# A gated S4D layer on one core: kernel tables finished in place in a wider tile, wider VectorE operations, tokens put in order on GpSimd

## The chip, the core and the metric

The kernel runs on one core of one Trainium2 chip. The metric is device microseconds for one execution; the time before is the median of three runs. TensorE (PE) does the matmuls, VectorE (DVE), ScalarE (ACT) and GpSimd (POOL) the elementwise work, and SyncE (SP), ACT and POOL issue the DMAs. All arithmetic is fp32; matmuls written on `F32R` tiles take one pass over the columns, and the others are plain fp32. To keep accuracy with `F32R`, an operand is split into a rounded part ("high") and the rest ("low"), and a product is made of high×high, high×low and low×high.

## What is computed

`x` is 2048 tokens of 576 channels. After a LayerNorm two branches run on the same `xn`, and their product is added to `x`:

```python
xn = layernorm(x)
s  = S4D(xn)                       # long convolution per channel
g  = silu(MLP(xn))                 # 576 -> 4608 -> 576, per token, with its own layernorm
return x + s * g

# S4D: the convolution kernel K[d, l], l = 0..2047, from 128 complex states per channel
A = -exp(log_A_real) + 1j * A_imag;  C = (C_real + 1j * C_imag) * dt
K = 2 * real(einsum("dn,dnl->dl", C, exp(A * dt * l)))
y = irfft(rfft(xn, 4096) * rfft(K, 4096))[:2048] + xn * D_skip

# MLP
h = gelu(layernorm(xn) @ w1 + b1);   out = h @ w2 + b2
```

## The kernel before

**The MLP is the frame.** The hidden width 4608 goes in 12 groups of 384, and the tokens in 4 blocks of 512; a *slot* is one block with one group, and there are 48 slots. A slot has 3 positions of layer 1 (`layer1`, L599, 13 or 14 matmuls of 512 columns each) and 8 of layer 2 (`layer2`, L662, 72 matmuls of 288 columns). Between the two, ACT takes the GELU (L635) and the high part (L638) and DVE the low part (L641, tile `hl`); after layer 2 DVE adds the block to `acc` (L672). The weights of the next group are split by ACT and DVE (L552, L549).

**The S4D branch is put between these matmuls.** The 576 channels go in 36 batches of 16 for the convolution kernel and in 6 chunks of 96 for the transform:

- `tables(b)`, one batch of 16 channels: tile `w` (2 x 16 x 65 columns, two buffers) takes a phase for 65 time steps per channel (DVE L897, L900, L906; ACT L903, L909), then its cosine and sine (ACT L914, L916). `mags` (L922) makes magnitudes in `mg`. `weigh` multiplies them: six operations of 512 columns write the single-buffered tiles `U` (2 x 16 x 32) and `v` (2 x 16 x 64) (L933, L935, L937, L939). The phase of batch b waits until the `weigh` of batch b-2 is done, and the first `weigh` of batch b until the outer product of batch b-1 is done.
- `kgen(b)`, the **outer product** (L978): 32 fp32 matmuls of 64 columns on 128x32 tiles of TensorE, weights from `U`, columns from `v`. It gives K at 2048 places for 16 channels, which ACT copies to `kt` (L983).
- `chunk(c)`, the transform in steps: `x1` (L1082, from the tokens), `k1` (L1113, from `kt`), four times `s2` (L1143, both at once), the pointwise complex product, two inverse steps (L1185), the last inverse step `i1` (L1211). Between them DVE transposes (L1090, L1121, L1196).
- `in_parts` splits the input of `x1` and `k1`: ACT high (L1058), DVE low (L1062). For `x1` both read the tile `xc` (32 tokens x 24 channels a partition) with tokens and channels exchanged, so that neighbours lie 96 bytes apart; for `k1` they read `kt` as it lies.
- The pointwise product in `s2`: `copy` (ACT L1152) takes the kernel's half of PSUM to `kk`; `prod` (DVE L1158) makes two products of 384 columns, and `sums` (L1164, L1165) a difference and a sum of 192 columns.

**Order.** `Order` is a planner that runs while the program is recorded. It has a time for each engine, a price for each step (`dve(n)`, `act(n)`, written-out numbers) and steps in lines, and it records steps in the order of its own times; the order on each engine is then fixed. Work that layer 2 waits for has a due time (`hidden_by`, `look_ahead`), and other work goes ahead of it only if it ends before that. `pe_turns` decides which S4D step goes to TensorE at a position of a slot. A step of a chunk is taken when its inputs have been ready for 0.4 us by the plan and, for `x1`, `k1` and `s2`, when some share of the mean distance between steps has passed.

**Company.** `ride` lets an outer product that is ready go right ahead of a step `x1`, `k1`, `s2` or `i1` (its *host*), in columns 384 to 511 of the host's PSUM tile (`lead`). An outer product that found no host goes alone once it has been ready for `ALONE` = 12 us, or 3 us when the next batch's sines are made and its due time (from 160 to 950 us, spread over the batches) has passed; in `pe_turns`:

```python
wait = ("sin", b + 1, 1) not in od.marks or od.t["PE"] < DUE[0] + b * (DUE[1] - DUE[0]) / NB
if b < NB - 1 and od.t["PE"] < h[1] + (ALONE if wait else 3.0):
    break
```

**A pair.** The last 64 rows of layer 1's input can be worked for two positions at once on two 64-row halves of TensorE (`pair`, L582). It is used at the end of a slot if an S4D step follows there and its operands are in time; it saves the two matmuls on `w1s` that the next slot would have.

Of the kernel before, what the change touches and what calls it, by code (L numbers as in the profile page):

```python
# [210 lines left out]
def mixer_kernel(ctx, tc, u, log_a_real, a_imag, c_real, c_imag, log_dt, d_skip, w1, b1, w2, b2,  # L211
# [38 lines left out]
    idp = sb.tile([P, P], F32, name="idp")  # L250
# [112 lines left out]

    def table_memory():

        t = [sb.tile([P, 2, SB, NV], F32, name="w", bufs=2) for _ in range(2)]
        t = [x.rearrange("p k c t -> p (k c t)") for x in t + [sb.tile([P, 2, SB, 64], F32, name="v")]]
        return [t[k // 3][:, k % 3 * D:(k % 3 + 1) * D] for k in range(8)]
# [401 lines left out]
    def params():  # L770
# [8 lines left out]
        dt = sb.tile([P, 2, SB, 32], F32, name="U").rearrange("p a b c -> p (a b c)")[:, :D]  # L779
# [108 lines left out]
    def tables(b):  # L888
# [5 lines left out]
        def phase(k):  # L894
            if k == 0:
                T["w"] = sb.tile([P, 2, SB, NV], F32, name="w", bufs=2)
                nc.vector.tensor_mul(T["w"][:, 1], bc(PAR[b][:, :, 0], 2, NV), bc(tv, 1, SB))  # L897
            else:
                u = T["w"][:, 1, :, 33:]
                nc.vector.tensor_add(u, u, bc(PAR[b][:, :, 1], 2, 32))  # L900
# [24 lines left out]
        def weigh(k, part):  # L925

            if k == 0 and part == 0:
                T["v"] = sb.tile([P, 2, SB, 64], F32, name="v")
                T["U"] = sb.tile([P, 2, SB, 32], F32, name="U")
                TAB[b] = (T["U"], T["v"])  # L930
            w, v, m = T["w"], T["v"], T["m"]
            if part == 0:
                nc.vector.tensor_mul(T["U"][:, k], w[:, k, :, 33:], m[:, :, 64:])  # L933
            elif part == 1:
                nc.vector.tensor_mul(v[:, k, :, :32], w[:, k, :, 32:0:-1], m[:, :, :32])  # L935
            elif k == 0:
                nc.vector.tensor_mul(v[:, k, :, 32:], w[:, k, :, :32], m[:, :, 32:64])  # L937
            else:
                nc.vector.scalar_tensor_tensor(v[:, k, :, 32:], w[:, k, :, :32], -1.0, m[:, :, 32:64],  # L939
# [6 lines left out]
                 step("DVE", dve(SB * NV), f(phase, 0), need=[("wu", b - 2, 1)] if b > 1 else []),  # L946
# [6 lines left out]
                + [step("DVE", dve(n), f(weigh, k, part), need=[("sin", b, k)] + ([("kg", b - 1)] if b else []),  # L953
                        mark=("wu", b, k) if part == 2 else None) for k in range(2) for part in range(3)])
# [10 lines left out]
    def kgen(b):  # L965
# [20 lines left out]
        return [step("PE", KG + 0.2, mm, need=need + [("wu", b, 1)], cv=1, mark=("kg", b)),  # L986
# [23 lines left out]
    def chunk(c):  # L1010
# [41 lines left out]
        def in_parts(which, i, get, m, need):  # L1052

            def high():
                a = sb.tile([P, 2, 4 * CH], F32R, name="pr").rearrange("p t c -> p (t c)")
                b = sb.tile([P, 2, 4 * CH], F32R, name="ys", bufs=2).rearrange("p t c -> p (t c)")
                PARTS2[which, i] = [t.rearrange("p (c b) -> p c b", b=m) for t in (a, b)]
                nc.scalar.activation(PARTS2[which, i][0], get(), AF.Copy)  # L1058

            def low():  # L1060
                a, b = PARTS2[which, i]
                nc.vector.tensor_sub(b, get(), a.bitcast(F32))  # L1062

            n = 768 if which == "k" else 2000
            four.append(step("ACT", act(n), high, need=need))
            four.append(step("DVE", dve(n), low, mark=(which + "p", c, i)))

        def x1(i):
# [641 lines left out]
```

## Time and profile before

| | |
|---|---|
| median of three runs | 1099.98 us (1099.77 to 1100.17) |
| span of the profiled execution | 1099.5 us |
| TensorE busy | 1090.1 us (99%) |
| VectorE busy | 920.5 us (84%) |
| ScalarE busy | 696.6 us (63%) |
| GpSimd busy | 184.6 us (17%) |
| DMA, mean over the span | 126 GB/s |

The times of runs are those of executions without the profiler; the trace is one profiled execution, and all places ("at 621 us") are in its own time. A row of a view names the source line, the engine, the operation, what it writes and reads, and the shape; in the views by groups there follow the count, busy time in us, mean ns of one, and the idle time of that engine just before with what ended it. In the timeline a row starts with the start time and the duration in us; equal neighbours are merged with their count. Matmuls overlap each other in their records, so the rate of TensorE is read from the starts of successive rows.

### The profile page before, as it was taken

To read this page: it belongs to the slowest core of one execution; us is meant where nothing else is said; L and a number is where in the kernel's file an instruction comes from. 1 tells how busy PE (TensorE), PEld (TensorE's weight loads), DVE (VectorE), ACT (ScalarE), POOL (GpSimd) and SP (SyncE) were. 2 spreads that over 40 slices of the span, in tenths; PEclk is the share of its full clock that TensorE was granted. 3 is DMA by queue.
4 is the path that set the end of the run, shared out by engine and by line. 5 is a ranking of instruction groups with operands and counts; after the bars stand their busy time and mean duration, and the time that the engine had idled before them with its cause. 6 is when DMAs were issued, how large, how long until landed. Compare 5 with 4: busy or idle time off the path is not lost.

```text
span 1099.5 us, 27206 instructions
## 1 busy us (share of the span) xinstructions
PE 1090.1 (99%) x11447; PEld 953.9 (87%) x11447; DVE 920.5 (84%) x1514; ACT 696.6 (63%) x1040; POOL 184.6 (17%) x254
## 2 busy tenths in 40 slices
PE   9999999999999999999999999999999999999997
PEld 7989899889888888888998888888888888888896
DVE  7798678979998899999999998898998986765356
ACT  6585699866666675676865857566675754325233
POOL 5566211170110100001100000000100012110220
PEclk9999999999999999999999999999999999999999
DMA  8746655734444152455623314242333426453453
GB/s 230 235 144 156 232 162 196 215 75 126 154 124 145 48 112 57 116 121 143 150 57 94 91 56 126 39 147 60 90 92 77 143 65 180 117 177 108 126 149 94
DMA packets 139683, 138.23 MB, mean 126 GB/s; under 512 B 88952, under 2 KB 105016, under 8 KB 138984
## 3 DMA queue, kind: packets, MB, share of 16 engines
q1 hardware_dynamic: 124664, 85.49, 29.5%
q0 software_dynamic: 14336, 50.12, 14.8%
q8 instruction: 89, 1.46, 0.6%
q10 hardware_dynamic: 560, 0.89, 0.3%
q14 instruction: 34, 0.28, 0.1%
HBM read 102.17 MB, written 36.63 MB: 126 GB/s over the span
## 4 chain that ended last, share of the span: by engine, by line
PE 96%; SPq 1%; DMA 1%; DVE 1%; issue 0%; ACT 0%; ACTq 0%; DVEq 0%
PE mxb L662 21%; PE mxa L662 21%; PE mxa L599 20%; PE mxb L599 20%; PE cv L1143 3%; PE cv L978 3%; PE cv L1185 2%; PE cv L1211 2%; PE cv L1113 1%; PE cv L1082 1%; DMA w<-in_A_u_dram 1%; SPq L791 1%; PE mxa L614 0%; SPq L383 0%; DMA acc<-in_A_u_dram 0%
## 5 line engine op out<-in xcount | busy, mean ns | idle before, releaser
L641 DVE TENSOR_TENSOR hl<-h,hh 128x512 fp32r<-128x512 f32 x144 | 99.1, 691 | 88.3 <-ACT hh L638 87.6
L662 PE MATMUL mxb<-w2h,hh 128*128 128x288 f32 x576 | 171.6, 298 | 0.0
L662 PE MATMUL mxa<-w2h,hh 128*128 128x288 f32 x573 | 170.8, 298 | 0.0
L662 PE MATMUL mxb<-w2h,hl 128*128 128x288 f32 x576 | 170.1, 295 | 0.3 <-DVE hl L641 0.3
L662 PE MATMUL mxb<-w2l,hh 128*128 128x288 f32 x576 | 169.5, 294 | 0.0
L662 PE MATMUL mxa<-w2h,hl 128*128 128x288 f32 x573 | 169.1, 295 | 0.0
L662 PE MATMUL mxa<-w2l,hh 128*128 128x288 f32 x573 | 168.6, 294 | 0.0
L635 ACT ACTIVATE h<-mxa,b1t 128x512 f32<-128x512 f32 x73 | 50.2, 688 | 111.8 <-PE mxa L599 110.1
L662 PEld LDWEIGHTS mxa<-w2h,hh 128*128 128x128 f32 x573 | 107.6, 188 | 6.6 <-issue 3.5
L662 PEld LDWEIGHTS mxb<-w2h,hh 128*128 128x128 f32 x576 | 108.1, 188 | 5.7 <-issue 1.5
L662 PEld LDWEIGHTS mxb<-w2l,hh 128*128 128x128 f32 x576 | 108.1, 188 | 0.6
L662 PEld LDWEIGHTS mxb<-w2h,hl 128*128 128x128 f32 x576 | 108.1, 188 | 0.5 <-DVE hl L641 0.5
L662 PEld LDWEIGHTS mxa<-w2l,hh 128*128 128x128 f32 x573 | 107.6, 188 | 0.6
L662 PEld LDWEIGHTS mxa<-w2h,hl 128*128 128x128 f32 x573 | 107.5, 188 | 0.0
L879 POOL DMA_DIRECT2D par<-par_s x36 | 27.8, 773 | 464.2 <-DVE mg L922 459.5
L638 ACT ACTIVATE hh<-h 128x512 fp32r<-128x512 f32 x144 | 90.6, 630 | 3.6
L635 ACT ACTIVATE h<-mxb,b1t 128x512 f32<-128x512 f32 x71 | 48.9, 689 | 68.9 <-PE mxb L599 66.5
L672 DVE TENSOR_TENSOR acc<-mxa,acc 128x576 f32<-128x576 f32 x87 | 65.5, 752 | 31.4 <-PE mxa L662 31.0
L672 DVE TENSOR_TENSOR acc<-mxb,acc 128x576 f32<-128x576 f32 x88 | 66.1, 752 | 16.0 <-PE mxb L662 15.5
L599 PE MATMUL mxa<-XH,w1h 128*128 128x512 f32 x284 | 79.1, 400 | 0.0
L599 PE MATMUL mxb<-XH,w1h 128*128 128x512 f32 x280 | 77.8, 399 | 0.0
L599 PE MATMUL mxa<-XL,w1h 128*128 128x512 f32 x284 | 76.1, 390 | 0.0
(261 smaller groups left out, 2485.9 us busy)
## 6 DMA issues: line engine op xcount, KB each, us to landing
raw<-in_B_w_dram SPq DMA_DIRECT2D x72, 288.0 KB, 3.5
raw<-in_B_w_dram SPq DMA_DIRECT2D x96, 192.0 KB, 3.8
par_s<-A POOLq DMA_DIRECT2D x4, 2160.0 KB, 8.2
par<-par_s POOLq DMA_DIRECT2D x36, 240.0 KB, 3.6
f2t<-f2q SPq DMA_DIRECT2D x24, 256.0 KB, 3.3
g2t<-g2p SPq DMA_DIRECT2D x24, 256.0 KB, 4.0
bias<-XR SPq DMA_DIRECT2D x42, 128.0 KB, 3.8
raw<-in_B_w_dram SPq DMA_DIRECT2D x48, 96.0 KB, 4.0
```

Of the source, the lines that this page charges most:

```text
L599: nc.tensor.matmul(q, a, b, start=j == 0 and i not in BEGUN, stop=j == len(ops) - 1, skip_group_check=True)
L635: nc.scalar.activation(t, q, AF.Gelu_apprx_tanh, bias=b1t[:, k:k + 1], scale=1.0)
L638: LAST[0] = nc.scalar.activation(hh[:, i], t, AF.Copy)
L641: nc.vector.tensor_sub(hl[:, i], t, hh[:, i].bitcast(F32))
L662: nc.tensor.matmul(q[:, dh, :288], a[:, i, c], b[:, i, d], start=i == 0 and k == 0 and not alone, stop=i == G - 1 and k == 2)
L672: nc.vector.tensor_add(o, q[:, dh:dh + n, :288], b)
L791: nc.sync.dma_start(r[32 * g:32 * g + 32].rearrange("c (b n) -> c b n", n=32), dram(src[k], 32 * g, [[N, 32], [32 * N, D // 32], [1, 32]]))
L879: nc.gpsimd.dma_start(PAR[b].rearrange("p (g i) k -> p g (i k)", g=4), dram(par_s, (b // 3 * 48 + b % 3 * 4) * NPAR, [[D * NPAR, P], [12 * ...
L978: nc.tensor.matmul(q[32 * g:32 * g + 32, i // 2, i % 2 * 64:i % 2 * 64 + 64], U[:, ri, 4 * g + i, :], v[:, ri, 4 * g + i, :], start=ri == ...
L1143: nc.tensor.matmul(Q[i][32 * q:32 * q + 32, f, 2 * ri:2 * ri + 2], m[r, 4 * i + q, 32 * ri:32 * ri + 32], A2[r, 4 * p + 2 * i + q // 2, :, ...
L1185: nc.tensor.matmul(QI[q // 2][64 * f:64 * f + 64, q % 2, i], MAT["g2t", p + i // 2][r, i % 2, f, ri], YS[p + i // 2][0][r, i % 2, ri, f], ...
L1211: nc.tensor.matmul(Q[h][64 * y:64 * y + 64, t], g1t.rearrange("p a e -> p (a e)"), A2[:, k:k + 2, 1].rearrange("p i d r -> p i r d"), star ...
```

## The change

- **One tile for the tables.** `w` becomes 2 x 16 x 97 columns with two buffers (`table_tile`); the phases and their cosines and sines stand in its last 65 columns, `weigh` writes its results into the same tile, and `U` and `v` are gone. The phase of batch b now waits for the outer product of batch b-2, and `weigh` no longer waits for one. The six operations of `weigh` become four: two of 1024 columns and two of 512.
- **Outer products** without a host wait 20 us by the plan (`ALONE`).
- **Wider operations.** The transposes after `x1` and `k1` take 24 channels at once (48 of 768 columns for 96 of 384). In `s2` the results of matmuls go to PSUM in another order (`ri::2`: two runs of 96 columns with 96 columns between them), `kk` gets a third, negated copy by one more ACT operation, and `prod` and `sums` become one operation each of 768 and 384 columns.
- **GpSimd orders tokens.** For `x1` a `tensor_copy` on POOL writes the exchanged tokens to a new tile `xt`; ACT high and DVE low read that as it lies.
- `idp` and the parameter tile `dt` take the memory of other tiles.

```diff
-    idp = sb.tile([P, P], F32, name="idp")
+    idp = sb.tile([P, 4, P], F32, name="f2t")[:, 0]
...
+    def table_tile():
+        return sb.tile([P, 2, SB, 32 + NV], F32, name="w", bufs=2)
...
             if k == 0:
-                T["w"] = sb.tile([P, 2, SB, NV], F32, name="w", bufs=2)
+                T["v"] = table_tile()
+                T["w"] = T["v"][:, :, :, 32:]
...
-        def weigh(k, part):
+        def weigh(part):
...
             if part == 0:
-                nc.vector.tensor_mul(T["U"][:, k], w[:, k, :, 33:], m[:, :, 64:])
+                nc.vector.tensor_mul(v[:, :, :, :32], w[:, :, :, 32:0:-1], bc(m[:, :, :32], 1, 2))
             elif part == 1:
-                nc.vector.tensor_mul(v[:, k, :, :32], w[:, k, :, 32:0:-1], m[:, :, :32])
-            elif k == 0:
-                nc.vector.tensor_mul(v[:, k, :, 32:], w[:, k, :, :32], m[:, :, 32:64])
+                nc.vector.tensor_mul(w[:, :, :, 33:], w[:, :, :, 33:], bc(m[:, :, 64:], 1, 2))
+            elif part == 2:
+                nc.vector.tensor_mul(w[:, 0, :, :32], w[:, 0, :, :32], m[:, :, 32:64])
...
-                 step("DVE", dve(SB * NV), f(phase, 0), need=[("wu", b - 2, 1)] if b > 1 else []),
+                 step("DVE", dve(SB * NV), f(phase, 0), need=[("kg", b - 2)] if b > 1 else []),
...
-                + [step("DVE", dve(n), f(weigh, k, part), need=[("sin", b, k)] + ([("kg", b - 1)] if b else []),
-                        mark=("wu", b, k) if part == 2 else None) for k in range(2) for part in range(3)])
+                + [step("DVE", dve((2, 2, 1, 1)[part] * n), f(weigh, part), need=[("sin", b, 1)],
+                        mark=("wu", b) if part == 3 else None) for part in range(4)])
...
+            def turn():
+                T["x"] = sb.tile([P, 24, m], F32, name="xt")
+                nc.gpsimd.tensor_copy(T["x"], get())
+
+            def source():
+                return get() if which == "k" else T["x"].rearrange("p c b -> p (c b)")
...
-            n = 768 if which == "k" else 2000
-            four.append(step("ACT", act(n), high, need=need))
-            four.append(step("DVE", dve(n), low, mark=(which + "p", c, i)))
+            if which == "x":
+                four.append(step("POOL", 2.3, turn, need=need))
+            four.append(step("ACT", act(768), high, need=need))
+            four.append(step("DVE", dve(768), low, mark=(which + "p", c, i)))
...
-                for e in range(2):
-                    c0 = 48 * i + d0 + 12 * e
-                    add("DVE", 0.65, lambda d0=d0, e=e, c0=c0: nc.vector.transpose(
-                        A2[:, :, 0, c0:c0 + 12].rearrange("p k d r -> p d k r"), Q[d0][:, e]), cv=-e)
+                c0 = 48 * i + d0
+                add("DVE", 0.9, lambda d0=d0, c0=c0: nc.vector.transpose(
+                    A2[:, :, 0, c0:c0 + 24].rearrange("p k d r -> p d k r"), Q[d0]), cv=-1)
...
-                                nc.tensor.matmul(Q[i][32 * q:32 * q + 32, f, 2 * ri:2 * ri + 2],
+                                nc.tensor.matmul(Q[i][32 * q:32 * q + 32, f, ri::2],
...
-                KK[i] = sb.tile([P, 2, 2, CH], F32, name="kk")
-                nc.scalar.activation(KK[i], Q[i][:, :, 1::2], AF.Copy)
+                KK[i] = sb.tile([P, 2, 3, CH], F32, name="kk")
+                nc.scalar.activation(KK[i][:, :, :2], Q[i][:, :, :1:-1], AF.Copy)
+                nc.scalar.activation(KK[i][:, :, 2], Q[i][:, :, 3], AF.Copy, scale=-1.0)
...
-                for t in range(2):
-                    nc.vector.tensor_mul(PR[i][:, t], bc(Q[i][:, t, 0::2], 2, 2), bc(KK[i][:, t], 1, 2))
+                nc.vector.tensor_mul(PR[i], bc(x, 2, 2), k)
...
-                nc.vector.tensor_sub(y[:, i, 0], x[:, :, 0, 0], x[:, :, 1, 1])
-                nc.vector.tensor_add(y[:, i, 1], x[:, :, 0, 1], x[:, :, 1, 0])
+                nc.vector.tensor_add(y[:, i].rearrange("p a t d -> p t a d"), x[:, :, :, :CH], x[:, :, :, CH:])
...
-    ALONE, DUE = 12.0, (160.0, 950.0)
+    ALONE, DUE = 20.0, (160.0, 950.0)
```

More of the change, by code (lines that the diff above doesn't have):

```diff
@@ L1119, in k1 @@
             add("PE", X1, mm, cv=2, mark=("k1", c, i), need=[("kp", c, i)] + ([("i1", c - 1)] if c and i == 0 else []))
[L1120 to L1124 removed]
+            for g in (0, 2):
+                add("DVE", 0.9, lambda g=g: nc.vector.transpose(
+                    A2[:, :, 1, 48 * i + 12 * g:48 * i + 12 * g + 24].rearrange("p k d r -> p d k r"), Q[g]), cv=-1)
         def s2(p):
@@ L1163, in sums @@
                 x, y = PR[i], Y[0]
-                nc.vector.tensor_sub(y[:, i, 0], x[:, :, 0, 0], x[:, :, 1, 1])
-                nc.vector.tensor_add(y[:, i, 1], x[:, :, 0, 1], x[:, :, 1, 0])
+                nc.vector.tensor_add(y[:, i].rearrange("p a t d -> p t a d"), x[:, :, :, :CH], x[:, :, :, CH:])
             for i in range(2):
-                two.append(step("ACT", act(4 * CH), lambda i=i: copy(i), need=[("s2", c, p)]))
-                two.append(step("DVE", 0.95, lambda i=i: prod(i), cv=-1))
-                two.append(step("DVE", 0.63, lambda i=i: sums(i), mark=("sum", c, p) if i else None))
+                two.append(step("ACT", act(4 * CH) + act(2 * CH), lambda i=i: copy(i), need=[("s2", c, p)]))
+                two.append(step("DVE", dve(8 * CH), lambda i=i: prod(i), cv=-1))
+                two.append(step("DVE", dve(4 * CH), lambda i=i: sums(i), mark=("sum", c, p) if i else None))
             if p % 2:
```

40 lines of the change are left out of this document (17 added, 23 removed).

## The prediction

> **What bounds the kernel now.** I read the page first, then the busy time by stretches of 100 us, then TensorE's timeline around single S4D steps.
>
> ```profile
> span 1099.5 us, 27206 instructions
> ...
> PE 1090.1 (99%) x11447; PEld 953.9 (87%) x11447; DVE 920.5 (84%) x1514; ACT 696.6 (63%) x1040; POOL 184.6 (17%) x254
> ...
> PE 96%; SPq 1%; DMA 1%; DVE 1%; issue 0%; ACT 0%; ACTq 0%; DVEq 0%
> ```
>
> ```profile
> 400.00:500.00 100.00, 100.00 (x1304) 87.00 (x1303) 94.48 (x155) 65.99 (x91) 3.00 (x4) 1.00 0.37 90
> ...
> 1000.00:1099.50 99.50, 93.14 (x737) 83.14 (x736) 56.96 (x91) 35.52 (x58) 17.02 (x27) 0.99 0.44 120
> ```
>
> The chain that ends last is TensorE for 96%. (The columns of the second view: the stretch and its length, then busy us of PE, of its weight load, of DVE, ACT and POOL, each with its count, the granted clock, the DMA's share and GB/s.) In its fullest stretch VectorE has 94.48 of 100 us, and TensorE misses nothing there. In all 1099.5 us TensorE is idle for 9.4: 6.4 of it in the last row, behind its last matmul, and 3.0 in all the rest, the start included. So this kernel ends when TensorE's list is through, and an engine beside it counts only if it makes TensorE wait. The rows for stalls in the middle are few; the largest is this one:
>
> ```profile
> 621.04 1.59 PE L1143 MATMUL cv<-A,f2t 64*32 64x192 f32 x61
> 623.22 0.53 PE L1143 MATMUL cv<-A,f2t 64*32 64x192 f32 x3 [0.59 <-issue]
> 623.67 0.40 PE L662 MATMUL mxb<-w2h,hh 128*128 128x288 f32 x1
> ```
>
> This `s2` takes 623.67-621.04 = 2.63 us. By its group's row (below: 39.1 us for 24 steps) one takes 1.63 with its tail in it, so about 1 us is a stop that no engine's work ended.
>
> **Part one, TensorE's list.** Set beside each other in program order, the two programs have the same number of matmuls, and the same number of each kind but for one more pair. What differs is their order. Before, 18 of the 36 outer products stand alone between matmuls of the MLP and 18 ahead of a host; afterwards it is 11 and 25. What that is worth is read from three places: an outer product alone, a `k1` alone, and both together.
>
> ```profile
> 152.53 0.39 PE L599 MATMUL mxa<-XR,w1s 128*128 128x512 f32 x1
> 152.84 1.10 PE L978 MATMUL cv<-v,U 128*32 128x64 f32 x64
> 153.88 0.73 PE L599 MATMUL mxb<-XH,w1h 128*128 128x512 f32 x2
> ...
> 262.65 0.62 PE L599 MATMUL mxb<-XH,w1l 128*128 128x512 f32 x2
> 263.10 0.39 PE L599 MATMUL mxb<-XR,w1r 128*128 128x512 f32 x1
> 263.42 0.64 PE L1113 MATMUL cv<-pr,f2t 32*128 32x384 f32 x8
> ...
> 264.70 0.40 PE L662 MATMUL mxa<-w2h,hh 128*128 128x288 f32 x1
> ...
> 284.89 0.39 PE L599 MATMUL mxa<-XR,w1s 128*128 128x512 f32 x1
> 285.21 1.10 PE L978 MATMUL cv<-v,U 128*32 128x64 f32 x64
> 286.24 0.63 PE L1113 MATMUL cv<-pr,f2t 32*128 32x384 f32 x8
> ...
> 287.52 0.40 PE L662 MATMUL mxb<-w2h,hh 128*128 128x288 f32 x1
> 287.76 0.29 PE L662 MATMUL mxb<-w2l,hh 128*128 128x288 f32 x1
> 287.89 0.29 PE L662 MATMUL mxb<-w2h,hl 128*128 128x288 f32 x1
> ```
>
> Alone: from the last MLP matmul's start to the next one's, 153.88-152.53 = 1.35, less the 0.23 that a matmul of layer 1 takes anyway ((263.10-262.65)/2), is 1.12; and the first pair of matmuls after it takes 0.73 where 0.62 is usual (row at 262.65), so 0.11 more: **1.23**. With a host: 287.52-284.89 = 2.63 for both, less 264.70-263.10 = 1.60 for the `k1` alone: **1.03**. Company is worth 0.20 us a time: one change of tile shape less. Seven more times: **-1.4 us**. Hosts of another kind change shape just as often, so I use 0.20 for all.
>
> The extra pair saves two matmuls of layer 1, 2 x 0.23 = 0.46, and costs:
>
> ```profile
> 230.87 0.50 PE L582 MATMUL mxa<-XR,w1s 64*128 64x512 f32 x1
> ...
> 231.30 0.49 PE L978 MATMUL cv<-v,U 128*32 128x64 f32 x20
> ```
>
> 0.43 (231.30-230.87), the entry being paid by the step behind it. Net 0.
>
> Two kinds of matmul change their addresses. Outer products read rows that start every 97 columns and no longer every 32 or 64; `s2` writes two runs of 96 columns instead of one of 192. No row of before shows either, so I bound them by what reading and writing of other forms costs at the same rate:
>
> ```profile
> L978 PE MATMUL cv<-v,U 128*32 128x64 f32 x2304 | 39.6, 221 | 0.0
> L1143 PE MATMUL cv<-A,f2t 64*32 64x192 f32 x1536 | 39.1, 332 | 0.6 <-issue 0.6
> ```
>
> An outer product streams 8 x 64 = 512 columns in 1.03 us, 2.0 ns each; an `s2` streams 4 x 192 = 768 columns in 1.63, 2.1 ns each, though it reads every second word and the other reads neighbours. Reading apart from reading together thus shows within 5%, and I bound both edits by that, 5% of 39.6 + 39.1: -4 to +4 us, with 0 as the value, since layer 2 writes 288 columns in 0.13 us (287.89-287.76), 0.45 ns each, so that at 2 ns writing has time to spare.
>
> **Part two, work beside it.** VectorE, from these rows:
>
> ```profile
> L933 DVE TENSOR_TENSOR U<-w,mg 128x512 f32<-128x512 f32 x72 | 49.3, 684 | 3.7 <-PE cv L978 2.3 <-ACT w L914 0.7
> L1158 DVE TENSOR_TENSOR pr<-cv,kk 128x384 f32<-128x384 f32 x96 | 48.7, 550 | 2.0 <-ACT kk L1152 1.8
> L922 DVE TENSOR_TENSOR mg<-par 128x1024 f32<-128x1024 f32 x36 | 44.0, 1223 | 0.7
> L1062 DVE TENSOR_TENSOR ys<-xc,pr 128x768 fp32r<-128x768 f32 x12 | 24.7, 2057 | 2.0 <-ACT pr L1058 2.0
> ...
> L1164 DVE TENSOR_TENSOR ys<-pr 128x192 f32<-128x192 f32 x48 | 17.0, 355 | 1.0
> L1062 DVE TENSOR_TENSOR ys<-kt,pr 128x768 fp32r<-128x768 f32 x12 | 11.1, 928 | 0.0
> ```
>
> `weigh`: 6 x 0.684 = 4.10 becomes 2 x 1.223 + 2 x 0.684 = 3.81, 36 times: -10. Products: 2 x 0.550 becomes one of 768 columns, 0.928, 48 times: -8. Sums: 2 x 0.355 becomes 0.550, 48 times: -8. Transposes, taken like the products since they are as wide: -8. Low parts of tokens: 2.057 becomes 0.928, 12 times: -14. In all about **-48 us of VectorE**, worth nothing at the end: TensorE was not waiting for it.
>
> ```profile
> L1058 ACT ACTIVATE pr<-xc 128x768 fp32r<-128x768 f32 x12 | 25.2, 2103 | 13.1 <-DMA xc<-xn_s 12.8 <-DVE w L900 0.3
> L1152 ACT ACTIVATE kk<-cv 128x384 f32<-128x384 f32 x48 | 23.1, 482 | 24.7 <-PE cv L1143 13.8 <-DVE pr L1158 10.9
> L1058 ACT ACTIVATE pr<-kt 128x768 fp32r<-128x768 f32 x12 | 10.1, 838 | 3.8 <-PE cv L1082 3.3 <-ACT w2h L552 0.3 <-PE cv L1113 0.3
> L914 ACT ACT_TABLE_LOAD x30 | 38.5, 1283 | 0.5
> ```
>
> ScalarE: high parts of tokens 2.10 to 0.84, 12 times: -15; the negated copy, at most 0.48 and, with half the columns, some 0.32 by my estimate, 48 times: +15; six more table loads at 1.283: +8. It has 37% of the span free.
>
> GpSimd has a new copy of 768 columns, 12 times, and the new wait chain is tokens landed, POOL copy, ACT high, DVE low, `x1`. POOL's copies of this form aren't in the trace; around it are
>
> ```profile
> L432 POOL TENSOR_SCALAR w<-w,mv,rs 128x576 f32<-128x576 f32 x6 | 16.5, 2755 | 17.4 <-ACT w2h L552 9.5 <-ACT h L635 7.8
> L549 POOL TENSOR_TENSOR w1l<-raw,w1h 128x384 fp32r<-128x384 f32 x2 | 2.0, 1018 | 0.1
> L1266 POOL MEMSET XL<- 128x512 f32 x1 | 0.5, 525 | 0.3 <-POOLq L1696 0.3
> ```
>
> From below, the memset's rate: 0.8 us. From above, the two-operand rate (2 x 1.018 = 2.04), slowed as the far-apart reading slows VectorE (2057 against 928): 4.5. I take the middle, **2.6**, near the tensor-with-scalars row (2.755 for 576). Behind it stand ACT's high part, and behind that on ACT the GELUs, for which layer 2 waits; on POOL the parameter loads of later batches. The old chain was 2.10 + 2.06 = 4.16 us, the new 2.6 + 0.84 + 0.93 = 4.37, so tokens are ready 0.2 later, against a slack that was smallest here:
>
> ```profile
> 933.18 2.05 DVE L1062 TENSOR_TENSOR ys<-xc,pr 128x768 fp32r<-128x768 f32 x1
> ...
> 936.37 0.62 PE L1082 MATMUL cv<-pr,f2t 64*128 64x384 f32 x4
> ```
>
> 936.37-935.23 = 1.14 us. It is hidden; without that cover it would cost 12 x 0.2 = 2.4.
>
> [...]
>
> The longer wait holds back what is queued behind an outer product: the phase of batch b+2, now waiting for it, and with the third product of each half chunk the `k1`. In the changed program's order the least distance from such a product to its `k1` is 54 matmuls of layer 2, some 7 us at 0.13; between lie one ACT copy, 0.84 and 0.93. No wait follows.
>
> **The sum.** The profiled execution has 1099.5; less 1.4 is 1098.1. The median of the runs, 1099.98, is 0.5 above that profile, and I keep the distance: **1098.6 us**. A difference under 0.2% (2.2 us) is about what can't be told from no change.
>
> **Rivals.** *A, the hand-over through GpSimd comes late* (slower, chance 0.10). It decides if the copy takes over 4.16 + 1.14 - 1.77 = 3.5 us. At 4.5 a token set is ready 2.1 later; if all 12 had the least slack that is 12 x 1.0 = 12 us, if half of them had it, 6: with the -1.4 some 1104 to 1110. For it speaks only the bound from above; against it that the plan gives the copy 2.3 us and sets `x1` after it.
>
> *B, TensorE's small stops go too* (faster, chance 0.17). If the lighter VectorE takes away the stop of 1 us at 621 and another like it, -2.4: 1097.6. Against it: that stop was not ended by VectorE.
>
> *C, the gap in what `s2` writes, or the new rows, slow the small matmuls* (slower, chance 0.04). It decides if a column takes longer to write than the 2.1 ns in which it comes. At the 5% above it is +4 - 1.4: 1102.5; if gaps doubled the write and with it the step, 24 x 1.63 = +39: 1138. I give each 0.02; against both speaks the 0.45 ns of layer 2. [...]
>
> *D, the change doesn't reach TensorE at all* (no change, within the forecast's class): the seven shapes saved are lost again to waits: 1100.0.
>
> **From this to the numbers.** The forecast with D has 0.69. Range: B's 1097.6 less another 0.6 below, 1097.0; above, C's lower part and the small end of A, 1102.4. Faster by over 2.2 us needs B: 0.17; slower A and C: 0.14; within: 0.69.
>
> **What would show it.** Right: L978 in 11 places alone, TensorE near 99%, VectorE near 870 us, ACT near 705, L599 and L662 with the same means, and the last matmul 1 to 2 us earlier. Wrong: the copy to `xt` over 3.5 us with `x1` waiting for `ys`; the mean of L1143 over 332 ns or of L978 over 221; waits of L662 for `hl`.

## The result, and the profile after

The changed kernel takes 1108.26 us (1108.11 to 1108.47 in four runs), beside 1100.08 for the kernel before (1099.77 to 1100.33): a ratio of 1.0073, 95% interval 1.0059 to 1.0087. It became slower, by 8.2 us in the medians.

The page of the changed kernel:

```profile
span 1106.3 us, 27046 instructions
...
PE 1090.7 (99%) x11447; PEld 954.3 (86%) x11447; DVE 912.8 (83%) x1298; ACT 701.1 (63%) x1094; POOL 210.6 (19%) x266
...
PE 88%; DVE 7%; ACT 2%; issue 2%; DMA 1%; SPq 0%; DVEq 0%; ACTq 0%
```

TensorE's busy time is the same, 1090.7 against 1090.1 us; what grew is the span around it. In the chain that ended last TensorE has 88% where it had 96%, and VectorE, at 1% before, has 7%. TensorE's own waits say where (columns: us in all, times, the longest):

```profile
PE mxa L601 <- ACT h L637: 4.5, 4, 1.4
...
PE mxa L601 <- DVE acc L674: 1.3, 1, 1.3
PE cv L979 <- DVE w L938: 1.1, 1, 1.1
```

`mxa` is a PSUM tile that layer 1 can't fill again until the GELU has read it (`h`) or layer 2's sum has left it (`acc`). I also added up, over the starts of all matmuls, what each distance is longer than the usual one of its kind in the trace of before; I call the sum *stops*. Before it is 2.0 us, of which 1.1 are the stop at 621 us; after, 9.9, in a dozen places of up to 1.6 us. Without the stops TensorE's list is 0.8 shorter (last matmul begun at 1099.99 against 1092.84: 7.15 later, of which 7.9 are stops). So TensorE's list did get shorter, and other engines made TensorE wait.

One stop with all engines in one timeline (start, duration):

```profile
368.57 3.20 DVE L940 SCALAR_TENSOR_TENSOR w<-w,mg 128x512 f32<-128x512 f32 x1
369.11 2.10 POOL L1059 COPY xt<-xc 128x768 f32<-128x768 f32 x1
371.81 1.23 DVE L925 TENSOR_TENSOR mg<-par 128x1024 f32<-128x1024 f32 x1
372.17 0.29 PE L664 MATMUL mxb<-w2h,hl 128*128 128x288 f32 x1
372.95 0.75 DVE L674 TENSOR_TENSOR acc<-mxa,acc 128x576 f32<-128x576 f32 x1
...
373.75 0.50 PE L601 MATMUL mxa<-XH,w1h 128*128 128x512 f32 x1 [1.28 <-DVE acc L674]
```

Read it from the end. TensorE starts layer 1 at 373.75, 1.58 us after its last matmul of layer 2 where 0.13 is usual, because `acc` came at 372.95. `acc` was late because on VectorE two operations stood ahead of it, and the first took 3.20 us. An operation of that shape takes 0.68. Inside its 3.20 us lies the whole copy on GpSimd. Here the same goes through ScalarE:

```profile
659.07 2.10 POOL L1059 COPY xt<-xc 128x768 f32<-128x768 f32 x1
659.12 3.17 DVE L909 TENSOR_TENSOR w<-w 128x1040 f32<-128x1040 f32 x1
662.32 1.09 ACT L912 ACTIVATE w<-w 128x1040 f32<-128x1040 f32 x1 [3.80 <-DVE w L909]
663.43 1.28 ACT L637 ACT_TABLE_LOAD   x1
663.66 0.39 PE L601 MATMUL mxb<-XR,w1s 128*128 128x512 f32 x1
664.73 0.69 ACT L637 ACTIVATE h<-mxa,b1t 128x512 f32<-128x512 f32 x1
...
665.47 0.72 PE L601 MATMUL mxa<-XH,w1h 128*128 128x512 f32 x2 [1.42 <-ACT h L637]
```

`L909` takes 3.17 in place of 1.23; ScalarE waits 3.80 us for it, and behind that stand a table load and the GELU that TensorE needs. The same pattern comes again at 803 us. In the groups of the changed kernel the stretched operations raise the means, while what the prediction had its eye on lies where it was foreseen:

```profile
L643 DVE TENSOR_TENSOR hl<-h,hh 128x512 fp32r<-128x512 f32 x144 | 102.8, 715 | 100.1 <-ACT hh L640 99.7
L909 DVE TENSOR_TENSOR w<-w 128x1040 f32<-128x1040 f32 x36 | 48.3, 1342 | 2.0 <-ACT w L906 2.0
L940 DVE SCALAR_TENSOR_TENSOR w<-w,mg 128x512 f32<-128x512 f32 x36 | 27.0, 751 | 0.0
L979 PE MATMUL cv<-w 128*32 128x64 f32 x2304 | 39.9, 220 | 1.3 <-DVE w L938 1.1 <-DVE w L940 0.2
L1150 PE MATMUL cv<-A,f2t 64*32 64x192 f32 x1536 | 38.5, 333 | 0.0
L1059 POOL COPY xt<-xc 128x768 f32<-128x768 f32 x12 | 27.5, 2291 | 53.2 <-DMA xc<-xn_s 38.9 <-DVE ys L1071 14.3
```

### The profile page after: what moved, and what is told of

Same layout as the page of the kernel before. It is cut to its first block, busy times and chain, and to the rows that moved or that the text cites. A ratio compares the mean times of both kernels' runs of the same rounds, so it can differ in the third digit from the quotient of the medians.

```text
span 1106.3 us, 27046 instructions
## 1 busy us (share of the span) xinstructions
PE 1090.7 (99%) x11447; PEld 954.3 (86%) x11447; DVE 912.8 (83%) x1298; ACT 701.1 (63%) x1094; POOL 210.6 (19%) x266
## 4 chain that ended last, share of the span: by engine, by line
PE 88%; DVE 7%; ACT 2%; issue 2%; DMA 1%; SPq 0%; DVEq 0%; ACTq 0%
PE mxb L664 19%; PE mxa L664 19%; PE mxa L601 19%; PE mxb L601 18%; PE cv L1150 3%; PE cv L979 3%; PE cv L1193 2%; PE cv L1122 1%; PE cv L1092 1%; DVE acc L674 1%; DVE mg L925 1%; DVE w L909 1%; PE cv L1219 1%; ACT L637 1%; DVE w L900 1%
## 5 line engine op out<-in xcount | busy, mean ns | idle before, releaser
L643 DVE TENSOR_TENSOR hl<-h,hh 128x512 fp32r<-128x512 f32 x144 | 102.8, 715 | 100.1 <-ACT hh L640 99.7
```

Of the source, the lines that this page charges most:

```text
L643: nc.vector.tensor_sub(hl[:, i], t, hh[:, i].bitcast(F32))
```

## The experiments

The theory from this trace: while GpSimd works, an operation of VectorE that reads two operands from SBUF is held until it ends; twelve copies of 2.1 to 2.7 us, each with a stretched operation, make VectorE late at places where the order has no room. It has two forms: only a GpSimd instruction that reads far apart holds (1a, where an expectation says so), or any instruction does, for its length (1b). Rivals: the copy delays only its own chain; the new order on TensorE is the cause; the wider operations or the new tiles are. The ratios are to runs of the kernel before on the same chip. *Stops* are counted as above; for the kernel in which TensorE itself reads far apart they are left out, since its own matmuls are slower there.

| kernel | us, median (range) | ratio to before, 95% interval | span | stops | VectorE busy |
|---|---|---|---|---|---|
| before (median of the runs; the rest from its one profiled execution) | 1099.98 | | 1099.5 | 2.0 | 920.5 |
| the change | 1108.26 (1108.11–1108.47) | 1.0073 (1.0059–1.0087) | 1106.3 | 9.9 | 912.8 |
| no copy, planned anew | 1102.40 (1101.99–1104.01) | 1.0021 (1.0011–1.0030) | 1100.6 | 2.2 | 904.3 |
| copy of neighbours | 1099.41 (1098.89–1100.18) | 0.9993 (0.9983–1.0002) | 1098.1 | 1.7 | 897.0 |
| before, with the copy added | 1120.18 (1118.60–1121.67) | 1.0176 (1.0159–1.0193) | 1119.8 | 18.3 | 934.1 |
| copy as a scaling | 1108.11 (1107.99–1108.66) | 1.0073 (1.0056–1.0089) | 1106.3 | 9.6 | 911.9 |
| copy in four pieces | 1104.92 (1104.80–1105.04) | 1.0042 (1.0027–1.0057) | 1103.3 | 6.6 | 906.4 |
| TensorE reads far apart | 1113.23 (1113.01–1113.57) | 1.0118 (1.0103–1.0133) | 1111.4 | | 893.5 |
| copy on ScalarE, order kept | 1103.88 (1103.30–1103.89) | 1.0034 (1.0021–1.0046) | 1102.1 | 5.3 | 891.7 |
| copy on ScalarE, planned | 1100.71 (1100.51–1102.21) | 1.0008 (0.9999–1.0017) | 1098.8 | 2.1 | 892.5 |
| no copy, order kept | 1105.99 (1105.66–1106.24) | 1.0054 (1.0040–1.0067) | 1104.5 | 7.6 | 904.2 |
| copy planned as VectorE's | 1116.22 (1115.83–1116.77) | 1.0148 (1.0130–1.0166) | 1114.0 | 7.5 | 906.8 |

### Without the copy, and with a short one

No copy at all; ScalarE and VectorE read the tokens far apart as before, and the planner makes a new order:

```diff
-                four.append(step("POOL", 2.3, turn, need=need))
...
             def source():
-                return get() if which == "k" else T["x"].rearrange("p c b -> p (c b)")
+                return get()
```

> The changed kernel without its GpSimd copy: ACT's high part and VectorE's low part read the tokens 96 bytes apart again (2.1 us each), and everything else of the change stays; the planner makes a new order, with 15 outer products alone instead of 11. Theory 1 (each of the 12 copies holds a VectorE operation for about 2 us, and TensorE stops for it): no VectorE operation far over its usual time, TensorE's stops near 2 us instead of 9.9, time 1099 to 1101. Theory 2 (the new order itself is too tight, with the table loads ahead of the GELU and wider operations, and the copies only stand near by): stops of 1.5 us stay, time 1105 to 1109.

It took 1102.40. The stops fall from 9.9 to 2.2 and no VectorE operation is stretched. But it is 2 us above before, and a little outside what I expected: TensorE's last matmul begins 1.1 us later than in the profile of before with the same stops, though only 15 outer products stand alone there and not 18. I have no single cause for that.

The next kernel keeps the order of every engine as in the change, and only what the copy reads differs: neighbours, and no longer words 96 bytes apart. The tokens are then not exchanged, so `x1` works on them in another order.

```diff
-                nc.gpsimd.tensor_copy(T["x"], get())
+                nc.gpsimd.tensor_copy(T["x"].rearrange("p c b -> p (c b)"), XC[i].rearrange("p b d -> p (b d)"))
```

> The changed kernel, with the order of every engine the same, but the GpSimd copy reads its 768 columns as they lie instead of 96 bytes apart (tokens and channels are not exchanged, so the S4D branch works on tokens in another order). Theory 1a (reading far apart is what holds VectorE): copies of 1 to 2 us, no VectorE operation stretched by more than 0.5 us, TensorE's stops near 2 us, time 1099 to 1101. Theory 1b (any copy of GpSimd holds VectorE for as long as it runs): VectorE operations stretched by about the copy's time, 1103 to 1108. Theory 2 (the order is too tight by itself): 1106 to 1109, stops at the same places, though no VectorE operation is stretched.

1099.41, so by the two medians **8.85 us of the 1108.26 hang on how twelve copies read their words**, and so on how long each of them runs (0.83 to 1.52 us here, 2.09 to 2.74 in the change) and holds. In the timeline of this kernel the place of the first stop looks like this:

```profile
368.31 0.74 DVE L940 SCALAR_TENSOR_TENSOR w<-w,mg 128x512 f32<-128x512 f32 x1
368.85 0.88 POOL L1059 COPY xt<-xc 128x768 f32<-128x768 f32 x1
369.09 1.73 DVE L925 TENSOR_TENSOR mg<-par 128x1024 f32<-128x1024 f32 x1
```

An operation is stretched here too, by 0.5 us in place of 2.5, and TensorE doesn't notice. In all, ten of the twelve copies stretch an operation, by 0.24 to 0.68 us, 5 us together. A copy of neighbours holds as well, then, only for less; that so short a hold is absorbed, and the time with it, I hadn't expected of form 1b, while form 1a has the time right and the holds wrong. By the medians the rest of the change takes 0.95 us off (1100.36 for before, beside it), and the interval includes no change.

### The copy alone, on the kernel before

Each token tile of the kernel before is copied onto itself, far apart, ahead of ScalarE's high part:

```diff
+            def turn():
+                nc.gpsimd.tensor_copy(get(), get())
+
             def high():
...
+            if which == "x":
+                four.append(step("POOL", 2.3, turn, need=need))
+                need = ()
```

> The kernel before, with one thing added: a GpSimd copy of each token tile onto itself, read and written 96 bytes apart, ahead of ACT's high part; nothing else of the change. Theory 1: 12 VectorE operations held for the length of a copy (2 to 4 us each), TensorE's stops up from 2.0 to 5 or more, time 1103 to 1112. Theory 2: VectorE held or not, the old order takes it, 1099.5 to 1101.5.

1120.18: more than twice the loss, without any of the other edits, and beyond the 1112 that the theory allowed. Nine operations of VectorE are stretched, by 0.6 to 2.9 us, 16 us in all. TensorE's waits of this kernel:

```profile
PE mxb L662 <- DVE acc L672: 7.6, 2, 6.8
PE mxa L662 <- DVE hl L641: 2.4, 3, 1.5
PE mxa L582 <- DVE acc L672: 1.4, 1, 1.4
```

The one of 6.8 us isn't a stretched operation. VectorE there waited 6.17 us for tokens of layer 1 (`row<-y_s`): SyncE began to issue their loads at 479.02 us, behind a load of the transform's matrices that had to wait 7.2 us for the chunk's `s2`, done at 478.16. So a delay can also pass through a chunk and a DMA queue and come due elsewhere. More was lost here than its length: from 488.3 to 495.1 us the granted clock was 0.50, where it had been 1.00, and the 22 matmuls of layer 2 behind the stop followed each other at 0.24 us in place of 0.13, some 2.3 us more. So the 1120.18 is not the price of the holds alone. The other stops are shorter and most wait for `acc`, `hl` or the table `v`.

### The hold by itself

A small kernel of its own, with nothing of the layer in it, runs GpSimd operations on 768 columns beside VectorE operations on 512 columns:

```python
def far():   G.tensor_copy(dst[:, :768].rearrange("p (d b) -> p d b", b=32), src[:, :768].rearrange("p (b d) -> p d b", d=24))
def near():  G.tensor_copy(dst[:, :768], src[:, :768])
def tt():    V.tensor_sub(c[:, :512], a[:, :512], b[:, :512])          # two inputs from SBUF
def tp():    V.tensor_add(c[:, :512], q, b[:, :512])                   # q lies in PSUM
def ts():    V.tensor_scalar(c[:, :512], a[:, :512], 2.0, 1.0, op0=OP.mult, op1=OP.add)
```

> Not the layer, but the disputed cost by itself: GpSimd operations on 768 columns while VectorE runs nine operations of 512 columns behind each other, three times each; the output is left as loaded tokens. Theory 1a: behind a copy that reads 96 bytes apart, one VectorE operation with two inputs from SBUF takes 2 us and more instead of 0.68, and none does behind a copy, a scaling or an addition of neighbours; operations with an input from PSUM or with one input are not held. Theory 1b: all copies of GpSimd hold VectorE. Rival: nothing is held here, and what the trace of the changed kernel shows has another cause (a semaphore, a DMA).

Rows of its timeline, each GpSimd copy with the VectorE operation that fell into it: a far copy with `tt`, a near one with `tt`, a far one with `tp`, a far one with `ts`:

```profile
71.75 2.58 POOL L36 COPY dst<-src 128x768 f32<-128x768 f32 x1 [0.64 <-DVE src L82]
72.42 2.46 DVE L54 TENSOR_TENSOR c<-a,b 128x512 f32<-128x512 f32 x1
...
47.36 1.33 POOL L40 COPY dst<-src 128x768 f32<-128x768 f32 x1 [0.64 <-DVE src L73]
48.03 1.19 DVE L54 TENSOR_TENSOR c<-a,b 128x512 f32<-128x512 f32 x1
...
74.97 2.58 POOL L36 COPY dst<-src 128x768 f32<-128x768 f32 x1 [0.64 <-DVE src L73]
75.64 0.69 DVE L57 TENSOR_TENSOR c<-q,b 128x512 f32<-128x512 f32 x1
...
86.04 2.31 POOL L36 COPY dst<-src 128x768 f32<-128x768 f32 x1 [0.37 <-DVE src L78]
86.44 2.19 DVE L60 TENSOR_SCALAR c<-a 128x512 f32<-128x512 f32 x1
```

Undisturbed, `tt` and `tp` take 0.69 and `ts` 0.43. So `tt` is held for 1.77 us, `ts`, which has only one input from SBUF, for 1.76, and `tp` not at all; transposes (0.71) weren't either, and ScalarE's copies kept their pace (six in 3.94 us each of three times, the first time beside the far copy). Beside the near copy the hold is 0.50, beside a scaling of neighbours (1.30) it is 0.50, and beside an addition of two inputs (2.28) it is 1.48. So form 1b is right, any of these instructions holds, and 1a is not. In each of the three rows with a hold the held operation ends 0.3 to 0.6 us after the copy does, and the price of one far copy is 1.77 us. GpSimd pays as well: the far copy takes 2.09 beside the transposes and 2.58 here, where a `tt` had begun 0.05 us before it and kept its 0.69.

A second kernel of that kind asked which form of the copy would hold VectorE less, by the time of eight `tt`:

```python
def pieces():      # four copies of 192 columns
def far_out():     # reads neighbours, writes far apart
def scalars():     # neighbours, scaled by a scalar in SBUF
def far_scalars(): # far apart, scaled by a scalar in SBUF
```

> The disputed cost by itself again, with other forms on GpSimd beside VectorE's two-input operations of 512 columns: the far copy in one piece (held 1.8 us in the first probe), the same in four pieces, a copy that writes far apart and reads neighbours, and a scaling with the scalars read from SBUF (as the token norms have it, which in the trace of before run beside VectorE), near and far; and VectorE's own copy beside the far copy. [...] The norms' form: 0 to 0.4 us of holding, if the form and not the length is what matters; 2 to 4 us if only its place in the trace of before was lucky. The output is loaded tokens.

With none held, eight `tt` would take about 4.9 us, by the 0.60 us from start to start of those behind the hold. They took 6.72 beside the far copy (2.42), 6.67 beside the four pieces (4.18 together), and 6.43 beside far writing (2.42). The scaled ones are the two informative rows, VectorE's first and then GpSimd's:

```profile
38.56 5.45 DVE L58 TENSOR_TENSOR c<-a,b 128x512 f32<-128x512 f32 x8
...
47.15 6.72 DVE L58 TENSOR_TENSOR c<-a,b 128x512 f32<-128x512 f32 x8
```

```profile
38.74 2.33 POOL L52 TENSOR_SCALAR dst<-src,one 128x768 f32<-128x768 f32 x1 [7.17 <-DVE src L65]
...
47.32 3.59 POOL L55 TENSOR_SCALAR dst<-src,one 128x768 f32<-128x768 f32 x1 [6.25 <-DVE src L65]
```

The scaling is 1.0 to 1.2 us longer than the copy of the same form (2.33 against 1.33, 3.59 against 2.42), and that part doesn't hold VectorE. In both rows the two `tt` that begin 0.4 and 1.0 us after the scaling take their usual 0.67 and 0.68; the next one is held to the scaling's end and takes 1.30 beside the near one and 2.57 beside the far one. The near form thus holds for 0.6 us, more than the 0 to 0.4 that I had expected, and the far one for 1.9, like the plain far copy. That fits with the profile of before, which gave no warning. Its long GpSimd operations were scalings of that near form (`L432`, 16 of them, 2.3 to 4.0 us), and of the VectorE operations beside them five were longer than usual, by 0.2 to 0.35 us.

### Other ways to exchange the tokens

The far scaling in the change itself, order kept:

```diff
-                nc.gpsimd.tensor_copy(T["x"], get())
+                nc.gpsimd.tensor_scalar(T["x"], get(), unit1, unit1, op0=OP.mult, op1=OP.mult)
```

> The changed kernel in the same order, with GpSimd's far copy done as a scaling by 1 with the scalars in SBUF. If that form leaves VectorE alone: no VectorE operation over 1 us late, TensorE's stops 2 to 4 us (the token chain is 1 to 2 us longer), time 1099 to 1103. If it holds VectorE for its 3 to 4 us like the copy: more stops than with the copy, 1110 to 1118.

1108.11, between the two ranges that I had given, with the stops in the same places: no better than the copy, as the probe had it, and not worse, though the operation has a median of 2.39 us (2.14 for the copy) and reaches 4.31. VectorE's busy time is nearly that of the change too (911.9), so it is the part that holds that counts, and not the length of the instruction.

In four pieces, order kept, so that VectorE can go in between:

```diff
-                nc.gpsimd.tensor_copy(T["x"], get())
+                for d in range(0, 24, 6):
+                    nc.gpsimd.tensor_copy(T["x"][:, d:d + 6], get()[:, d:d + 6])
```

> The changed kernel in the same order, with the far copy in four instructions of 192 columns each. The theory that an instruction of GpSimd keeps VectorE out until its end: holdings of up to 0.6 us each in place of one of 2 us, several for each token tile; if VectorE's operations get in between them, stops of TensorE at 3 to 6 us and 1101 to 1105; if the pieces follow each other without a gap for VectorE, 2 us of holding again and 1107 to 1109.

1104.92. VectorE's busy time falls by 6.4 us and the stops by 3.3, though the copies together are longer. Some operations still were held through most of the four: `L909` twice took 2.9 where 1.23 is usual.

No exchange at all; the matmuls of `x1` read their columns 96 bytes apart:

```diff
-                PARTS2[which, i] = [T[k].rearrange("p (c b) -> p c b", b=m) for k in "ab"]
+                PARTS2[which, i] = [T[k].rearrange("p (c b) -> p c b", b=m) if which == "k" else
+                                    T[k].rearrange("p (b c) -> p c b", c=24) for k in "ab"]
```

> The changed kernel without any ordering of tokens on an engine: ACT and VectorE split the tokens as they lie, and the matmuls of x1 read their columns 96 bytes apart. GpSimd is left out, and the planner makes a new order with 15 outer products alone. If TensorE reads far apart at its usual rate: x1 takes 1.25 us as before, no VectorE operation is held, stops near 2 us, time 1098.5 to 1101. If it reads them at half the rate: 12 x 1.25 = 15 us more, 1113 to 1117.

1113.23. TensorE pays for it itself. The group of `x1` in this kernel, and in the change:

```profile
L1091 PE MATMUL cv<-pr,f2t 64*128 64x384 f32 x96 | 20.6, 513 | 0.0
```

```profile
L1092 PE MATMUL cv<-pr,f2t 64*128 64x384 f32 x96 | 13.3, 353 | 0.0
```

By the starts of the matmuls, twelve `x1` take 25.4 us in place of the 14.9 of the kernel before: 0.87 more each, and 10.4 of the 12.9 us that were lost. The order is a new one here, with 15 outer products alone, and where the other 2.5 us went I haven't traced.

### Is it GpSimd, or any time that the order doesn't know of?

The same far copy on ScalarE, at the place that the change's order had for GpSimd's; TensorE's and VectorE's orders stay:

```diff
-                nc.gpsimd.tensor_copy(T["x"], get())
+                nc.scalar.activation(T["x"], get(), AF.Copy)
```

> The same copy with the same far-apart reading, done by ScalarE and not by GpSimd, put where the plan had the GpSimd copy; TensorE's and VectorE's orders are the same as in the changed kernel, and ScalarE has 12 operations of about 2.1 us more. The probe showed ScalarE unhindered beside a copy and VectorE unhindered by ScalarE. Theory (a running GpSimd instruction holds VectorE's two-input operations): no VectorE operation is stretched, so the stops behind late sines, sums and tables go, but 2.1 us now stand ahead of GELUs on ScalarE in 12 places, some of which TensorE will meet: 1098.5 to 1102. Rival (far-apart copying of the tokens late in the chain is what costs, whoever does it, or the change's order and tile reuse): 1106 to 1109, with VectorE operations of 2 to 4 us as in the changed kernel.

And the same with ScalarE's price told to the planner, which then places the copy:

```diff
-                four.append(step("POOL", 2.3, turn, need=need))
+                four.append(step("ACT", act(2000), turn, need=need))
```

> The same, with ScalarE's price of the copy told to the planner, which puts GELUs and other work around it; 11 outer products alone. Theory: as before less the stops behind ScalarE: 1098 to 1100.5, a little below or level with the kernel before (its list of matmuls is some 1.4 us shorter), no VectorE operation stretched. Rival: 1106 to 1109.

With the order kept 1103.88, between what the theory gave (up to 1102) and what the rival gave (from 1106); planned 1100.71, 0.2 above the range that I gave, with 13 outer products alone in its trace and not 11. VectorE's busy time is the cleanest measure of the hold: with the same operations in the same order it is 891.7 us beside ScalarE's copies and 912.8 beside GpSimd's, **21.1 us held, 1.8 for each copy**. The busy time of the first of these two kernels, and two of its groups, to be read against those of the change (1342 and 715 ns):

```profile
PE 1090.1 (99%) x11447; PEld 954.3 (87%) x11447; DVE 891.7 (81%) x1298; ACT 724.0 (66%) x1106; POOL 183.7 (17%) x254
...
L909 DVE TENSOR_TENSOR w<-w 128x1040 f32<-128x1040 f32 x36 | 44.4, 1233 | 2.0 <-ACT w L906 2.0
...
L643 DVE TENSOR_TENSOR hl<-h,hh 128x512 fp32r<-128x512 f32 x144 | 99.0, 689 | 106.8 <-ACT hh L640 106.2
```

But with the order kept it still stops TensorE for 5.3 us. Its largest stop, on ScalarE and TensorE, shows why:

```profile
376.91 2.10 ACT L1059 ACTIVATE xt<-xc 128x768 f32<-128x768 f32 x1
...
379.02 1.28 ACT L637 ACT_TABLE_LOAD   x1
379.20 0.39 PE L601 MATMUL mxb<-XR,w1s 128*128 128x512 f32 x1
...
380.32 0.69 ACT L637 ACTIVATE h<-mxa,b1t 128x512 f32<-128x512 f32 x1
```

The copy stands ahead of the GELU, and the order was made without it. When the planner knows, the stops are 2.1 us.

The next one takes the copy out but keeps the change's order, so that ScalarE and VectorE read far apart, with 1.1 to 1.3 us more for each operation than the plan has:

```diff
             if which == "x":
-                four.append(step("POOL", 2.3, turn, need=need))
+                four.append(step("POOL", 2.3, lambda: None, need=need))
```

> The changed kernel without the GpSimd copy, but with the orders of TensorE, VectorE and ScalarE left as they are in the changed kernel (the plan keeps a place of 2.3 us and records nothing there); ScalarE and VectorE read the tokens 96 bytes apart as before, 2.10 and 2.06 us in place of 0.84 and 0.93, without the plan knowing it. Theory (the loss is the holding by GpSimd, the new order costs nothing): no VectorE operation is stretched; 12 x 1.1 us more on VectorE, which stands in no GELU's way for long; 1098.5 to 1101. Rival (the new order is itself worse, as the run without the copy at 1102.40 could mean): 1101.5 to 1104.

1105.99, outside what both theories gave, with 7.6 us of stops and none of the twelve holds. So the holding by GpSimd isn't the only way to lose this time: **work that the order doesn't know of costs TensorE, on whatever engine it falls.** With the order the same in all of them, these are the us that the plan didn't have against the stops: 5.3 held, 1.7; 14.7 held (four pieces), 6.6; 21.1 held, 9.9; 25 on ScalarE, 5.3; 15 on ScalarE and 13 on VectorE, 7.6. (Held is VectorE's busy time above 891.7.)

Last, the GpSimd copy entered in the plan as VectorE's work:

```diff
-                four.append(step("POOL", 2.3, turn, need=need))
+                four.append(step("DVE", 2.3, turn, need=need))
```

> The changed kernel with the same GpSimd copy, but entered in the plan as 2.3 us of VectorE, so that the order leaves room on VectorE where the copy is recorded; it still runs on GpSimd, and starts when its tokens and its tile are there, not at a planned time. The order on TensorE becomes another one, with 16 outer products alone, not 11 (some 5 x 0.1 to 0.2 us more). Theory (a delay costs where the plan does not know of it): VectorE's operations are still stretched by some 1.5 to 1.8 us each, 15 to 20 us in all, but stops of TensorE fall to 2 to 5 us: 1100.5 to 1103.5. Rival (a held VectorE costs by itself, wherever it is held): stops stay at 8 to 10 us, 1107 to 1110.

1116.22, a miss on the slow side for both theories. VectorE is still held for 15.1 us (906.8 less 891.7), the stops are 7.5, and the largest group of them waits for other operations than before:

```profile
PE mxa L664 <- DVE hl L643: 2.5, 6, 0.7
```

The plan reserved a place on VectorE, but nothing ties the copy to that place; it starts when its tokens are there. What the change didn't have lies behind the last matmul: that begins at 1099.8 as in the change (1100.0), but the span goes on for 14.2 us behind it and not for 6.3. The last inverse step comes at 1063 and not at 1042, and the last load of its result, a piece of the chain that ended last, lands at 1105.0:

```profile
1100.47 4.57 DMA A<-s_s
```

So this run doesn't show whether an order that really knew of the hold would be free of stops; that stays open.

## Why the prediction was wrong

**TensorE bounds the kernel, and its list gets shorter: right in kind, the size off.** Eleven outer products stand alone in the trace, as forecast. Seven shape changes less are worth 0.8 us by the starts of the matmuls with the stops taken out, both in the change and in the copy of neighbours, so 0.11 each and not 0.20, if all of it is theirs.

**The new addresses are free: right.** A matmul of the outer product has 220 ns (221), one of `s2` 333 (332). From the first start to the next step's, an outer product takes 1.03 us in both kernels and an `s2` 1.53 after 1.55 (medians). Rival C is out.

**VectorE's lighter work is worth nothing: right, and it was smaller than forecast.** With nothing held it is 891.7 us, 29 less than before and not 48. One reason is in a row that I had quoted: 96 products of 0.550 would be 52.8 us, and the row says 48.7, since the records of successive operations overlap. The products of 768 columns have 45.6 us where nothing is held (the copy on ScalarE, order kept), so they saved 3 and not 8. ScalarE came to 701.1 (705 expected).

**The GpSimd copy is hidden: this step failed.** Its own price was nearly right: 2.29 us in the mean (2.09 to 2.74), 2.6 assumed. Its chain was right too: `x1` waited 0.2 us for its tokens in all. What I left out, and so put at nothing, is what the copy does to *VectorE*: twelve holds, 21.1 us in all, and with them TensorE's stops went from 2.0 to 9.9 us. I priced the copy as work on an idle engine, with a wait chain behind it, and never asked which operations of another engine it would hold. I thought only of the tokens as late, while the sines of a batch, the sums of layer 2 and the tables of an outer product came late. The twelve holds are shown by the probe and by VectorE's busy time; operation by operation, the change and the copy on ScalarE have the same VectorE order, and just twelve operations are longer in the change by over 0.1 us, one under each copy, by 0.55 to 3.02. That the holds are the cause is shown by the copy of neighbours, which has the same order and the same twelve instructions and takes 1099.41, and by the scaling: its instructions are longer than the copies, VectorE's busy time is nearly the same, and so is the kernel's time.

**"TensorE was not waiting for VectorE" was read too far.** It says that VectorE's time can shrink for nothing. I took from it that time can also be added for nothing. But the spare time of VectorE lies where the planner left it, and the order is fixed: TensorE's stops grew in every run that added unplanned time, but for the one with 5 us.

**The sum started from the wrong distance.** In the changed kernels of this study an execution's own time is its span plus 1.7 to 1.9 us (1108.11 with 1106.3, 1099.87 with 1098.1), and a later run of the kernel before with a span of 1099.5 took 1101.27. The profile of before thus belongs to an execution of about 1101.3, 1.3 above the median. The stop of 1 us at 621 may be most of that; there is no second trace of the kernel before that could show it. The distance of 0.5 between profile and median was that of one execution and couldn't be carried over. For the copy of neighbours, which is the change without the loss, the sum's 1098.1 is what its span has, though in other parts (the list -0.8, stops -0.3, the end -0.3); its median is 1099.41, so the forecast of 1098.6 was 0.8 too low even there.

**Rival A** gave 1104 to 1110 and the time lies in it, but it isn't what happened: the copy never took the 3.5 us from which that rival decides. **Rival B** had one thing right: the stop at 621 us isn't in the profile after. But it may have belonged to that one execution and not to the kernel, by the 1.3 us above. The longer wait for company made no stop that I found.

## What to carry to other kernels

Before moving work to an idle engine, look for the operations of the neighbour that will run beside it, and price one hold for each instruction, here 1.8 us for a copy of 2.1 to 2.7. In a kernel whose order is fixed ahead, slack is not the idle share but the room behind each operation that the order was made with; an edit that lengthens operations has to be told to the planner, or it is paid for at the bound engine (here 0.2 to 0.5 us for each us beyond the first five). If a cheap variant of the new operation exists that leaves the order as it is, run it first: it separates what an instruction does from what the order does.

## What the hardware showed that I had not expected

- The hold takes operations with one input too: fp32 `tensor_scalar`, 2.19 us in place of 0.43, and VectorE's plain copy, 2.30 in place of 0.41. Operations with an input in PSUM (0.69) and transposes (0.71) pass beside the same copy.
- An operation that had begun before the copy can be held as well. In the change, on VectorE and GpSimd, with 1.22 us the usual duration of the first:

```profile
936.26 4.23 DVE L936 TENSOR_TENSOR w<-w,mg 128x1024 f32<-128x1024 f32 x1
```

```profile
937.30 2.09 POOL L1059 COPY xt<-xc 128x768 f32<-128x768 f32 x1
```

  It had run for 1.04 us when the copy began, and lost 3.0, more than the copy's length. In the first probe a `tt` that had begun 0.05 us before the far copy kept its 0.69; why it is otherwise here isn't settled. GpSimd issued DMAs right up to the copy, which may have had a part in it. Alone they don't hold: 171 VectorE operations of this trace fall beside such issues and no other GpSimd work, and none is over 0.1 us longer than usual.
- TensorE's moving operand isn't free of its step: 96 bytes apart cost `x1` 70% more, 2.1 us in place of 1.2.
- GpSimd is slowed by the far step whether it reads or writes with it: 2.42 us both ways in the second probe. In the first the near copy took 1.33 beside `tt`; beside VectorE operations that it doesn't hold, the far copy took 2.09 and the near one 0.83.
